# An attention block on one core: GpSimd's memsets of three groups split and placed later, the fourth query block ahead of the next group's keys

## The chip, the core and the metric

The kernel runs on one core of a Trainium2 chip. The metric is the time of one execution on the device, in microseconds. The core has five engines with instruction queues of their own: TensorE (PE, matrix products; its weight loads are listed as PEld), VectorE (DVE), ScalarE (ACT), GpSimd (POOL) and SyncE (SP, which here only issues DMAs). Each engine works through its queue in order; engines wait for each other by semaphores alone.

## What is computed

Multi-head attention with its projections, for 2048 tokens of width 448 and 16 heads of 28 (inputs and output in bf16):

```
qkv = (x @ wqkv).reshape(B, S, 3, H, Dh).transpose(2, 0, 3, 1, 4)
q, k, v = qkv
scores = einsum("bhqd,bhkd->bhqk", q, k) * Dh ** -0.5
p = softmax(scores, axis=-1)
o = einsum("bhqk,bhkd->bhqd", p, v)
return o.transpose(0, 2, 1, 3).reshape(B, S, D) @ wo
```

## The kernel before

**Tiles and windows.** The 16 heads are four groups (g) of four, the queries four blocks (c) of 512. A pair (g, c) is a window w = 4g + c, of which there are 16. A window has 16 rows (128 keys each), a row four score tiles of 128 x 512, one for each head: 1024 tiles in all. Window 0 and window 1 are each cut in two: first four rows of each (tiles 0 to 31), then the other twelve rows of each (to tile 127). Window 2 starts at tile 128, window 3 at 192, and group 1 at 256.

**What becomes of a tile.** PE computes the scores (line 875, `emit_S`). A softmax bound is folded into the product by extra rows of the keys (from NK) and of the queries (from QP), so no maximum is searched. Then there are three ways to the exponential:

- ACT takes two tiles at a time from a PA bank (PSUM has two PA banks) with one instruction, line 1295, into PTA.
- DVE and POOL share a tile from a PD bank (three, and the PO bank at times): DVE makes DU (line 1076) and DV (1079), POOL the product DG (1082), DVE the result PTD (1095). This is `start_tile`; the text calls DG a product.
- POOL makes a tile nearly alone: DVE copies it to SG (1008) and POOL takes six instructions (1015, 1018, 1021, 1023, 1025, 1038). This is `start_g`. Such tiles are taken 10 to 13 rows ahead of the others (`ahead`, LA = 10), and only where their queries and keys are there already.

PE then adds the products with the values into PO (line 1140), where a column of ones in the values (VA) also gives the sum of the exponentials; windows are normalised by way of a small DMA (RRB) and POOL (line 975), and multiplied with `wo`. Values of group g lie in VA[g]: 32 columns a head, of which every eighth is set to 1.0 by a memset of 128 x 256 elements. VA[0]'s memset is on DVE (line 326), those of VA[1] to VA[3] are on POOL (line 459), in one operation `va_ones`.

**The start.** DMAs bring the key weights WK (ACT's queue), x in three blocks XS, the query weights WQ, WV, and the first 512 rows of x transposed (SP's queue). DVE copies WK into a padded form WKP (line 388, `pad_w`), ACT does so for WQ (389). PE transposes XS (424), DVE and ACT bring the transposes to SBUF as XT (435, 437). PE then projects keys (532, `task_K`) and queries (662, `task_Q`) of the first block, ACT and DVE evacuate them (676, 548, 682 to 688), and the first scores and the first exponential follow.

**Who sets the order.** The order of all queues is written out by a planner in the kernel file: a list scheduler that keeps a model time. Operations (`Op`) have an engine, a modelled duration, dependencies, a priority (smaller first) and a condition `elig`, mostly on `pos[0]`, the number of score tiles issued so far. Whatever is ready on a free engine with the smallest priority comes next (`try_static`; for PE `try_pe`). Only the order is taken from it: on the chip an instruction starts when its queue has come to it and its semaphores allow. An operation without dependencies, such as `va_ones`, thus runs as soon as the queue reaches it. `DLAT` and `QLAT` are the modelled times from issue to landing of the key and the query moves (with 0.3 or 0.6 added for the keys), `KSP` the distance in tiles between the projections of the next group's four key blocks, `QPR` what is taken off a query block's priority.

For the first group, key moves are KB<-KB (line 591) and KB<-NK (601); for later groups 613 and 623. A query block w from 2 on is projected into a free bank, evacuated by DVE (672), made absolute (701; for group 0 also scaled, 705), and moved by two DMAs QB<-QB (710) and four QB<-QP (716). The block of w = 3 (the fourth) has priority 168 before the change, and may start at tile 131. The key blocks of group 1 have 56, 92, 128 and 164, and may start at tiles 2, 54, 106 and 158.

Behind `va_ones` stands `halves` (two small memsets, 463 and 464, and two small tensor_scalars, 466), also for POOL, from tile 8 on.

Of the kernel before, what the change touches and what calls it, by code (L numbers as in the profile page):

```python
# [21 lines left out]
RS = 8  # L22
NR = 128 // RS
G = 4
# [29 lines left out]
EVK = 0.66  # L54
RED = 0.59
DISS = 0.6
DLAT = 1.4
QLAT = 2.6
WINDOW = 3.4
BAR = 3600.0  # L60
BAR2 = 1700.0
# [23 lines left out]
def kernel(  # L85
# [7 lines left out]
    nc = tc.nc  # L93
# [21 lines left out]
    NG = 3  # L115
    GMAX = 1
    UK = 30
    KSP = 52
    PGX = 0
    GDEC = 4  # L120
    LA = 10
# [30 lines left out]
    QPR = 100  # L152
# [27 lines left out]
    KP0 = -4395  # L180
    KP1 = -4000
    VE = 16
    UV = 4
    BW = (-1, 2, 0)
    THF = (0, 1, 0, 0)
# [90 lines left out]
    def va_rows(g):  # L276
        return VA[g][:].rearrange("p j h (m e) -> p (j h m) e", e=RS)
# [53 lines left out]
    pos = [0]  # L331
# [7 lines left out]
    def add(op):  # L339
        static[op.eng].append(op)  # L340
        return op

    def bank_task():
        return {"slot": None}

    def acq_d(task, early=False, urgent=1e9):
        def f(t):
            if task["slot"] is not None:
                return True
            free = [s for s in ([o_slot] + d_slots if early or pos[0] >= min(urgent, NT - NTAIL) else [o_slot]) if s.free_at <= t + 1e-9]  # L350
            if not free:
                return False
            s = free[-1]
            s.free_at = 1e18
            task["slot"] = s
            return True
        return f
# [17 lines left out]
    def at(n):  # L375
        return lambda t: pos[0] >= n
# [32 lines left out]
    for b in range(NQC - XBAR):  # L409
        xs_in = add(Op("SP", 0.01, None, prio=-2000 + b, lat=XLAT[b]))  # L410
        for hf in range(2):
# [7 lines left out]
            def tr(b=b, hf=hf, tv=tv, tv2=tv2):  # L419
                for c2 in range(2):  # L420
                    for t in range(TPC):
# [5 lines left out]
                         elig=None if 2 * b + hf < 2 + TE else lambda t: len(k0mm) == 2 * CC and all(o.end is not None for o in k0mm),  # L427
# [15 lines left out]
            else:  # L443
                evo = add(Op(eng, 0.655 if eng == "DVE" else 0.905, ev, deps=[tro], prio=(EVP[b] if b else -5000) + 10 * b + hf,
                             elig=None if b == 0 or eng == 'ACT' or not BW[b] else lambda t, b=b: len(qb0) == HG and qb0[BW[b] - 1].end is not None))
# [8 lines left out]
            nc.sync.dma_start(out=WO[e::RS, :, :],  # L454
                              in_=bass.AP(wo.tensor, wo.offset + e * D, [[(RS - 1) * D, NR], [HG * Dh * D, G], [1, D]]))

    def va_ones():
        for g in range(1, G):
            nc.gpsimd.memset(va_rows(g)[:, :, RS - 1:RS], 1.0)
    add(Op("POOL", 0.9, va_ones, prio=-50, elig=lambda t: pos[0] >= 8))  # L460

    def halves():
        nc.gpsimd.memset(negm[:], 0.0)
# [15 lines left out]
    for g in range(1, G):  # L479
        for (WP, nm, off) in ((WKP, "k", D), (WQP, "q", 0)):  # L480
            def ld(g=g, WP=WP, off=off):
                for cc in range(CC):
# [5 lines left out]
                                      elig=None if first else (lambda t, g=g, nm=nm: pos[0] >= (30 if nm == "q" and g == 1 else (g - 2) * 256 + 120 + 40 * (nm == "q"))), lat=PLT))  # L488
# [29 lines left out]
    def task_K(g, sc):  # L518
# [6 lines left out]
        else:  # L525
            task = bank_task()
            acq = acq_d(task, urgent=(g - 1) * 4 * WT + (sc + 1) * KSP - UK)
            elig = at((g - 1) * 4 * WT + sc * KSP + 2)
            prio = due
# [47 lines left out]
    def task_kmax(g):  # L577
# [7 lines left out]
        if g == 0:  # L585
# [3 lines left out]
            for n, (c0, c1) in enumerate(KCH):  # L589
                for i in range(HG):  # L590
                    o = add(Op("SP", DISS, (lambda i=i, c0=c0, c1=c1: nc.sync.dma_start(
                        out=KB[0][i // 2][HP * SI[i]:HP * (SI[i] + 1), c0 * QW:c1 * QW],
                        in_=KB[1][0][HP * SI[i]:HP * (SI[i] + 1), c0 * QW:c1 * QW])),
                        deps=[k0ev[sc] for sc in range(c0, c1)], prio=-2000 + 20 * n + i, lat=DLAT + 0.3))
                    k0mv.append(o)
# [3 lines left out]
            def rep0(i, c0, c1):  # L599
                st = SI[i] ^ 1  # L600
                nc.sync.dma_start(out=KB[0][i // 2][HP * st:HP * (st + 1), c0 * QW:c1 * QW].rearrange("p (r q) -> p r q", q=P),
                                  in_=NK[0][HP * SI[i]:HP * (SI[i] + 1), None, :].to_broadcast([HP, (c1 - c0) * QW // P, P]))
            for n, (c0, c1) in enumerate(RCH):
                for i in range(HG):
                    o = add(Op("SP", DISS + 0.07, (lambda i=i, c0=c0, c1=c1: rep0(i, c0, c1)), deps=[nk],
                               prio=(-1990 + 20 * n if c0 else -300) + 0.1 * i, lat=DLAT + 0.6, elig=None if c0 else lambda t: pos[0] >= NF * FB * HG + 4))
                    for c in range(c0, c1):
# [4 lines left out]
        for st in (1, 3):  # L612
            o = add(Op("SP", DISS, (lambda st=st: nc.sync.dma_start(
                out=KB[g % 2][1][HP * st:HP * (st + 1), c0 * QW:S], in_=KB[g % 2][0][HP * st:HP * (st + 1), c0 * QW:S])),
                deps=[kev[(g, sc, 0)] for sc in range(c0, NQC)], prio=due + 0.01 * st, lat=DLAT + 0.3))
            deps.append(o)
# [3 lines left out]
        def rep_out(i, c0):  # L620
            st = SI[i] ^ 1
            n = (S - c0 * QW) // P
            nc.sync.dma_start(out=KB[g % 2][i // 2][HP * st:HP * (st + 1), c0 * QW:S].rearrange("p (r q) -> p r q", q=P),
                              in_=NK[g][HP * SI[i]:HP * (SI[i] + 1), None, :].to_broadcast([HP, n, P]))
        nk = add(Op("POOL", 0.25, lambda: nc.gpsimd.tensor_scalar(
            out=NK[g][:], in0=maskm[:, 0:P], scalar1=KMAX[g][:, 0:1], scalar2=0.0, op0=ALU.mult, op1=ALU.add), deps=[m], prio=prio + 0.2, elig=elig))
        for i in (2, 3, 0, 1):
            o = add(Op("SP", DISS + 0.07, (lambda i=i: rep_out(i, c0)), deps=[nk] + ([deps[i]] if i < 2 else []),
                       prio=due + 0.3 + 0.001 * i, lat=DLAT + 0.6))
            for c in range(c0, NQC):  # L630
# [6 lines left out]
    def task_Q(g, c):  # L637
        due = (g * 4 + c) * WT - 24
        n = qabs_n[0] % 2
        qabs_n[0] += 1  # L640
        w = g * 4 + c
        if w == 0:
            task = {"slot": d_slots[1]}
            acq = lambda t: xt_half[1].done(t)
            elig = None
            prio = -4500
        else:
            task = bank_task()
            acq = acq_d(task, urgent=w * WT - UQ)
            elig = at((w - 1) * WT + 3 - (QEA if w > 3 else 0))  # L650
            prio = due - (QPR if w > 3 else 0)
            if w < NF:
                task = {"slot": d_slots[2]}
                acq = lambda t: xt_half[2].done(t)
                elig = None
                prio = Q1P
            elif w == NF:
                acq = acq_d(task, urgent=Q2U)
                elig = at(Q2E)
                prio = 20  # L660
# [12 lines left out]
        if w < NF:  # L673
# [17 lines left out]
            for i in range(HG):  # L691
                o = bound(qb, i, KPART[0], [ab, kmaxop[0][0], e1], pq + (20 if i < 2 else 40) + 0.01 * i)
                if w == 0:
# [5 lines left out]
                    elig=elig if w < NQB else (lambda t: pos[0] >= ((w - NQB + 1) * WT if w - NQB >= NF else NF * FB * HG + (w - NQB + 1) * (WT - FB * HG)))))  # L699
# [9 lines left out]
        for st in (1, 3):  # L709
            mvs[st] = add(Op("SP", DISS, (lambda st=st: nc.sync.dma_start(  # L710
                out=qb[1][HP * st:HP * (st + 1), :], in_=qb[0][HP * st:HP * (st + 1), :])),
                deps=[ev], prio=(Q1M if w < NF else prio - 100) + 0.1 * st, lat=QLAT))
        mine = []
        for i in range(HG):
            st = SI[i]
            o = add(Op("SP", DISS, (lambda i=i, st=st: nc.sync.dma_start(
                out=qb[i // 2][HP * (st ^ 1):HP * ((st ^ 1) + 1), :], in_=QP[n][HP * st:HP * (st + 1), :])),
                deps=[ab] + ([mvs[st ^ 1]] if st in (0, 2) else []), prio=(Q1M + 1 if w < NF else prio - 99) + 0.1 * i, lat=QLAT))
            mine.append(o)
# [3 lines left out]
    def task_V(g, jq):  # L723
        due = g * 4 * WT + jq * TPC * HG - 12 + (FB * HG * (NF - 1) if g == 0 and jq else 0)
        task = bank_task()
        early = False
        elig = at(VE + jq * 5 if g == 0 else (g - 1) * 4 * WT + jq * WT + 4)
        prio = due
        ap = lambda: bank(task)[:]

        def mm(jj):
            for cc in range(CC):
                nc.tensor.matmul(out=ap()[:, jj * GW:(jj + 1) * GW], lhsT=XT[jq][cc // 2][0:CK, cc % 2, jj * P:(jj + 1) * P],  # L733
                                 rhs=WV[:, cc, g * GW:(g + 1) * GW], start=(cc == 0), stop=(cc == CC - 1))
        ops = []
        for jj in range(TPC):
            ops.append(add(Op("PE", 0.27, (lambda jj=jj: mm(jj)), deps=(xt_done[jq] + [wvin]) if jj == 0 else [ops[-1]],
                              prio=prio + 0.001 * jj, kind="W", elig=elig, acq=acq_d(task, early, urgent=due - UV if g == 0 else (g - 1) * 4 * WT + (jq + 1) * WT + 32) if jj == 0 else None,
                              lat=0.0 if jj < TPC - 1 else PLAT)))
# [13 lines left out]
        if g == 0:  # L753
            hot.append((ops[0], due - UV))

# [3 lines left out]
    def open_when(slot, ops):  # L759
# [3 lines left out]
        for o in ops:  # L763
            prev = o.after
            o.after = (lambda t, prev=prev: (prev(t) if prev else None, f(t)))
    task_Q(0, 0)
    open_when(a_slots[0], [xt_half[3]])
    a_slots[1].free_at = 0.0
# [5 lines left out]
    for c in range(1, NQC):  # L774
        task_Q(0, c)
    for g in range(1, G):
        for sc in range(NQC):
            task_K(g, sc)
        task_kmax(g)
        for c in range(NQC):  # L780
            task_Q(g, c)
        for jq in range(NQC):
            task_V(g, jq)
# [556 lines left out]
    while True:  # L1340
        if not times:
            break
        t = heapq.heappop(times)
# [76 lines left out]
    g = G - 1  # L1420
# [43 lines left out]
```

## Time and profile before

| what | value |
|---|---|
| time, median of 3 runs | 414.0 us (413.88 to 415.25) |
| time of the profiled execution | 415.08 us |
| its span in the profile | 413.3 us |
| granted PE clock, mean | 0.989 |
| busy: ACT / DVE / PE / POOL | 395.2 / 382.9 / 360.2 / 340.5 us |
| exponentials on ACT (line 1295) | 422, 1170 ns mean, 16.14 us to 404.54 us |
| products on POOL (line 1082) | 155, 1154 ns mean |
| tiles that POOL makes nearly alone | 26 |

The span is the time that the profile covers. Records of neighbouring instructions of an engine overlap by some hundred ns, so a mean of 1170 ns doesn't mean that one starts each 1170 ns. The page cuts the span in 40 slices of 10.3 us and gives busy tenths. In a windows table each row is a stretch, followed by its length, busy time (and count) of PE, PEld, DVE, ACT, POOL, then the granted PE clock as a share of full speed, the DMA share and GB/s. In the waits, an engine's instruction stands left of the arrow and what it waited for right of it, with the total, the number and the longest. In the timelines and the chain, the first number is the start and the second the duration.

### The profile page before, as it was taken

The page shows a single profiled execution, that of the slowest core. Times are in us where ns is not written, and L with a number is a line of the kernel's source. Part 1 is how long each engine was busy: PE and PEld are TensorE (multiplying, and loading weights), DVE is VectorE, ACT ScalarE, POOL GpSimd, SP SyncE. Part 2 cuts the span into 40 slices and gives each one's busy share as a digit, 9 for nine tenths or more (in the row PEclk, how much of TensorE's full clock was granted, in tenths as well). Part 3 has the DMA queues.
Part 4 walks back from the last instruction along what each step waited for, and adds up shares of the span by engine and source line. Part 5 has one row for each costly group of instructions (what it writes and reads, how often), then busy time and mean ns, then how long its engine had stood idle before and what let it go on. Part 6 is the DMA issues. An engine that isn't in the chain of part 4 may idle for free.

```text
span 413.3 us, 7565 instructions
## 1 busy us (share of the span) xinstructions
PE 360.2 (87%) x2591; PEld 120.9 (29%) x2602; DVE 382.9 (93%) x664; ACT 395.2 (96%) x434; POOL 340.5 (82%) x365
## 2 busy tenths in 40 slices
PE   5999989888898989889898988989798888889995
PEld 2543223222323232232323223232322222222231
DVE  6796899999999999999999999899999999998983
ACT  2799999999999999999999999999999999999993
POOL 6026998879999999899888989978998997989870
PEclk9799999999999999999999999999999999999998
DMA  9233213122101011032101001023100001010112
GB/s 230 22 71 48 55 24 58 22 71 51 52 17 32 21 33 11 15 74 56 48 21 31 3 14 52 12 56 70 34 21 6 26 5 48 2 51 2 51 71 90
DMA packets 36870, 17.30 MB, mean 42 GB/s; under 512 B 29216, under 2 KB 33568, under 8 KB 36832
## 3 DMA queue, kind: packets, MB, share of 16 engines
q1 hardware_dynamic: 36224, 16.61, 17.0%
q8 instruction: 20, 0.33, 0.3%
q10 hardware_dynamic: 608, 0.22, 0.2%
q14 instruction: 18, 0.15, 0.1%
HBM read 6.91 MB, written 2.33 MB: 22 GB/s over the span
## 4 chain that ended last, share of the span: by engine, by line
ACT 36%; DVE 28%; PE 14%; POOL 9%; issue 6%; DMA 4%; SPq 1%; DVEq 0%; POOLq 0%; ACTq 0%
ACT PTA L1295 36%; DVE PTD L1095 7%; DVE DU L1076 7%; DVE DV L1079 7%; PE PA L875 5%; POOL DG L1082 5%; PE PO L1140 3%; DMA RRB<-SCR 2%; POOL GV L1021 1%; DVE SG L1008 1%; PE PD L875 1%; DMA WK<-in_wqkv_dram 1%; POOL OT L975 1%; PE PD L817 1%; DVE QB L672 1%
## 5 line engine op out<-in xcount | busy, mean ns | idle before, releaser
L1295 ACT ACTIVATE PTA<-PA 128x1024 bf16<-128x1024 f32 x422 | 387.7, 1170 | 1.0 <-PE PA L875 0.9
L1082 POOL TENSOR_TENSOR DG<-DV,DU 128x512 f16<-128x512 f16 x155 | 177.0, 1154 | 40.0 <-DVE DV L1079 31.8
L875 PE MATMUL PA<-QB,KB 64*128 64x512 bf16 x843 | 168.9, 380 | 36.4 <-ACT PTA L1295 33.4
L875 PEld LDWEIGHTS <-KB 64*128 64x128 bf16 x1024 | 64.6, 93 | 176.9 <-issue 169.2
L1095 DVE SCALAR_TENSOR_TENSOR PTD<-PD,DG 128x512 uint16<-128x512 f32 x155 | 104.5, 682 | 5.1 <-POOL DG L1082 4.4
L1076 DVE TENSOR_SCALAR DU<-PD 128x512 f16<-128x512 uint16 x155 | 103.0, 681 | 5.0 <-PE PD L875 4.6
L1079 DVE SCALAR_TENSOR_TENSOR DV<-PD,DU 128x512 f16<-128x512 uint16 x155 | 103.7, 682 | 1.0
L1140 PE MATMUL PO<-PTA,VA 128*32 128x512 bf16 x843 | 86.7, 386 | 0.2
L875 PE MATMUL PD<-QB,KB 64*128 64x512 bf16 x181 | 65.9, 377 | 3.0 <-DVE PTD L1095 1.3
L1140 PE MATMUL PO<-PTD,VA 128*32 128x512 bf16 x181 | 52.1, 387 | 0.0
L1140 PEld LDWEIGHTS <-VA 128*32 128x32 bf16 x1024 | 19.7, 94 | 51.5 <-issue 51.1
L1025 POOL TENSOR_TENSOR SG<-SG,GU 128x512 f32<-128x512 f32 x26 | 30.0, 1155 | 2.1 <-DVE QP L701 0.8
L1021 POOL TENSOR_TENSOR GV<-GE,GU 128x512 f16<-128x512 f32 x26 | 30.1, 1157 | 1.5 <-DVE QP L701 0.7
L1023 POOL TENSOR_TENSOR GU<-GV,GU 128x512 f16<-128x512 f16 x26 | 30.0, 1154 | 1.3 <-DVE QP L701 0.4
L1015 POOL TENSOR_SCALAR GU<-SG 128x512 f16<-128x512 uint16 x26 | 16.1, 617 | 7.2 <-DVE SG L1008 3.3
L975 POOL TENSOR_TENSOR OT<-OSB,RRB 128x512 bf16<-128x512 f32 x15 | 19.0, 1269 | 3.1 <-DMA RRB<-SCR 3.1
L1008 DVE COPY SG<-PD 128x512 f32<-128x512 f32 x26 | 17.7, 680 | 3.4 <-PE PD L875 3.4
L662 PE MATMUL PO<-XT,WQP 112*128 112x512 bf16 x56 | 18.1, 385 | 1.0 <-DVE OSB L960 0.6
L733 PEld LDWEIGHTS <-XT 112*128 112x128 bf16 x256 | 13.9, 98 | 13.1 <-issue 12.8
L1018 POOL TENSOR_SCALAR GE<-SG 128x512 f32<-128x512 uint16 x26 | 16.1, 618 | 2.1
L1038 POOL TENSOR_SCALAR PTD<-SG 128x512 uint16<-128x512 f32 x26 | 16.1, 619 | 1.5 <-PE PD L875 0.6
L733 PE MATMUL PO<-WV,XT 112*128 112x112 bf16 x192 | 15.5, 214 | 0.9 <-DVE QB L672 0.5
(108 smaller groups left out, 206.6 us busy)
## 6 DMA issues: line engine op xcount, KB each, us to landing
RRB<-SCR SPq DMA_DIRECT2D x15, 256.0 KB, 3.3
QB<-QP SPq DMA_DIRECT2D x56, 32.0 KB, 1.8
KB<-NK SPq DMA_DIRECT2D x12, 128.0 KB, 2.7
XS<-in_x_dram SPq DMA_DIRECT2D x3, 448.0 KB, 4.7
QB<-QB SPq DMA_DIRECT2D x28, 32.0 KB, 1.8
out_dram<-XS SPq DMA_DIRECT2D x2, 448.0 KB, 2.9
KB<-KB SPq DMA_DIRECT2D x6, 128.0 KB, 2.3
RRB<-RR SPq DMA_DIRECT2D x2, 256.0 KB, 3.4
```

The lines of the kernel that those rows point to most:

```text
L733: nc.tensor.matmul(out=ap()[:, jj * GW:(jj + 1) * GW], lhsT=XT[jq][cc // 2][0:CK, cc % 2, jj * P:(jj + 1) * P], rhs=WV[:, cc, g * GW:(g + ...
L875: nc.tensor.matmul(out=ap, lhsT=KB[g % 2][i // 2][a:a + 64, j * P:(j + 1) * P], rhs=QB[w % NQB][i // 2][a:a + 64, :], start=True, stop=Tru ...
L975: o5 = add(Op("POOL", 1.22, lambda: nc.gpsimd.tensor_tensor(out=OT[g][c][:], in0=OSB[b][:], in1=RRB[b][:], op=ALU.mult), deps=o4, prio=-10 ...
L1021: g3 = add(Op("POOL", PTT, lambda: nc.gpsimd.tensor_tensor(out=GV[:], in0=GE[:], in1=GU[:], op=ALU.mult), deps=[g2], prio=prio + 2, kind=" ...
L1023: g4 = add(Op("POOL", PTT, lambda: nc.gpsimd.tensor_tensor(out=GU[:], in0=GV[:], in1=GU[:], op=ALU.mult), deps=[g3], prio=prio + 3, kind=" ...
L1025: g5 = add(Op("POOL", PST, lambda: nc.gpsimd.tensor_tensor(out=X[:], in0=X[:], in1=GU[:], op=ALU.add), deps=[g4], prio=prio + 4, kind="g", ...
L1076: p1 = add(Op("DVE", P1, lambda: nc.vector.tensor_scalar(out=DU[b][:], in0=lo, scalar1=SIG / 65536, scalar2=SIG * (SS - 0.5), op0=ALU.mult ...
L1079: p2 = add(Op("DVE", P1, lambda: nc.vector.scalar_tensor_tensor(out=DV[b][:], in0=lo, scalar=65536 * (SS - 0.5 + CE / C3), in1=DU[b][:], o ...
L1082: gq = add(Op("POOL", PTT, lambda: nc.gpsimd.tensor_tensor(out=DG[b][:], in0=DV[b][:], in1=DU[b][:], op=ALU.mult), deps=[p2], prio=n, kind ...
L1095: f = add(Op("DVE", P1, lambda: nc.vector.scalar_tensor_tensor(out=PTD[st["s"].idx][:].bitcast(U16), in0=PX[slot.idx][:], scalar=EBITS + C ...
L1140: nc.tensor.matmul(out=PO[HP * st:HP * (st + 1), :], lhsT=VA[g][:, j, st, :], rhs=r["p"][i][1](), start=first, stop=last, tile_position=(0 ...
L1295: nc.scalar.activation(out=PTA[pslot.idx][:, 0:len(ns) * QW], in_=PA[s.idx][:, 0:len(ns) * QW], func=ACT.Exp, bias=ACT_BIAS, scale=ACT_SCALE)
```

## The change

Three things are edited. The memsets of VA[1], VA[2] and VA[3] become three operations, each with a modelled duration of 1.17 instead of 0.9 for all, which may start when 24, 48 and 72 score tiles are issued instead of 8. The query block w = 3 gets 100 taken off its priority, as later ones had already (68 instead of 168). And three constants of the planner are new: DLAT 2.1 instead of 1.4, QLAT 2.0 instead of 2.6, KSP 60 instead of 52, so that the key blocks of group 1 may start at tiles 2, 62, 122 and 182.

```diff
-DLAT = 1.4
-QLAT = 2.6
+DLAT = 2.1
+QLAT = 2.0
...
-    KSP = 52
+    KSP = 60
...
+    VON = 24
...
-    def va_ones():
-        for g in range(1, G):
-            nc.gpsimd.memset(va_rows(g)[:, :, RS - 1:RS], 1.0)
-    add(Op("POOL", 0.9, va_ones, prio=-50, elig=lambda t: pos[0] >= 8))
+    for g in range(1, G):
+        add(Op("POOL", 1.17, lambda g=g: nc.gpsimd.memset(va_rows(g)[:, :, RS - 1:RS], 1.0), prio=-50 + g, elig=lambda t, g=g: pos[0] >= VON * g))
...
-            prio = due - (QPR if w > 3 else 0)
+            prio = due - (QPR if w > 2 else 0)
```

## The prediction

> **What bounds the kernel now.** I read the page first, for the engine that has no slack.
>
> ```profile
> PE 360.2 (87%) x2591; PEld 120.9 (29%) x2602; DVE 382.9 (93%) x664; ACT 395.2 (96%) x434; POOL 340.5 (82%) x365
> ...
> ACT  2799999999999999999999999999999999999993
> POOL 6026998879999999899888989978998997989870
> PEclk9799999999999999999999999999999999999998
> ```
>
> ScalarE (ACT) is full from the third slice to the last but one. The waits of ACT, longest first, show where its idle time is:
>
> ```profile
> ACT QB L676 <- PE PD L662: 6.3, 1, 6.3
> ...
> ACT PTA L1295 <- PE PA L875: 0.9, 2, 0.5
> ```
>
> Once the exponentials (L1295) run, they wait for 0.9 us in all. They begin at 16.14 and end at 404.54, 422 of them, so one each 0.920 us. The span is therefore: start (16.1) + exponentials (388.4) + tail (8.8). A change pays only if it moves the first exponential, the number of exponentials, or the tail. So I looked at the start next, in the chain of waits in order of time:
>
> ```profile
> 0.74 4.31 DMA WK<-in_wqkv_dram
> 5.04 0.21 issue
> 5.25 0.38 DVE WKP L388
> 5.63 2.73 issue
> 8.37 0.68 DVE XT L435
> 9.05 0.04 issue
> 9.09 1.01 PE PD L532 x2
> ```
>
> The padded key weights arrive, VectorE (DVE) copies them, and then 2.73 us pass with no named wait before the next copy. The timelines of DVE and of GpSimd (POOL) for 4.6 to 9 us (start, duration, instruction) say what went on:
>
> ```profile
> 5.25 3.19 DVE L388 COPY WKP<-WK 112x448 bf16<-112x448 bf16 x1 [0.77 <-DMA WK<-in_wqkv_dram]
> ```
>
> ```profile
> 4.64 3.51 POOL L459 MEMSET VA<- 128x256 bf16 x3
> 7.73 0.47 POOL L463 MEMSET negm<- 128x64 bf16 x1
> 8.02 0.30 POOL L464 MEMSET FW<- 128x128 bf16 x1
> 8.29 0.37 POOL L466 TENSOR_SCALAR negm<-maskm 128x16 bf16<-128x16 bf16 x2
> ```
>
> L388 copies SBUF to SBUF and takes 3.19 us. ACT does the same shape (L389) in 0.56, and L684 on DVE, a 128x512 copy with POOL idle, takes 0.29. It ends at 8.44, 0.29 us after the third memset of VA (8.15). So the three memsets, which nobody needs yet, hold up the first link of the start. There is a second price: TensorE (PE) has nothing from 5.93 to 9.09, and the windows table shows its granted clock fall.
>
> ```profile
> 8.00:8.50 0.50, 0.00 (x0) 0.00 (x1) 0.50 (x2) 0.00 (x0) 0.50 (x5) 0.94 1.17 224
> 8.50:9.00 0.50, 0.00 (x0) 0.10 (x1) 0.50 (x2) 0.00 (x0) 0.16 (x1) 0.50 2.24 194
> ...
> 15.00:15.50 0.50, 0.50 (x10) 0.50 (x9) 0.47 (x2) 0.50 (x1) 0.00 (x0) 0.74 0.00 0
> ```
>
> The clock (third number from the end) is half from about 8.44 to 15.26 (0.94 and 0.74 as shares of their half microseconds). The whole preparation of the first scores runs in that stretch.
>
> **The change, part by part.**
>
> *Memsets.* By the rule in the code, the first of the three is placed once 24 score tiles are issued. Before the first PD score matmul (25.80) PE has issued 22; the next pair passes 24, 2 us before the first product (28.20). So I read VON = 24 as: memset 1 still stands ahead of the first product in POOL's queue, memsets 2 and 3 behind some. Nothing in front of memset 1 waits for data, so it runs early, but now after the four small instructions (L463, L464, L466 twice). These take 0.93 us from the start of the first to the end of the last (7.73 to 8.66), so from 4.64 to at latest 5.57. In the old run the copy got through among just these four (it ended at 8.44, they at 8.66). I take it that it does so again, ahead of memset 1: end 5.57 + 0.29 = 5.86, 2.58 us earlier.
>
> Then, link by link. The XT copy starts at 5.79, the first projection matmul at 6.5 instead of 9.09. PE's gap is then 5.93 to 6.5, and I take the clock to stay full. The eight projection matmuls took 9.09 to 12.66 (0.43 each and a gap); at full clock two matmuls of L532 at 19.05 start 0.21 apart, so they end at about 6.5 + 8 x 0.21 = 8.2, with 0.2 for the second XT copy 8.4: 4.3 earlier. The 32 transposes behind them in PE's queue took 3.09 (12.66 to 15.75); at the rate of the last eight (0.53) 2.12, so they end at 10.5. Their data is there: the last XS load lands 6.5 us after its issue at about 2.2, at 8.7. On ACT the way from QB (12.70) to the end of the second KB (15.64) is 2.94 us of its own work: 8.44 + 2.94 = 11.4. DVE's bounds come out 2.0 us behind QB's start (14.67), now 10.4. First scores at 10.6, first exponential at the latest of these, 11.4 instead of 16.14: 4.7 less. Behind it everything shifts alike, if the loads are there: WV landed at 9.9 and the DMA share is 0 from 13.5 on, while the last key projection would run at 16 instead of 20.8. I keep 4.6. Bounds of this part: 0, if the stall was not the memsets' doing, and 5.0, if the copy passes all four small ones. If the cover of the later steps is gone, late next are ACT's own four instructions ahead of the first exponential, which no earlier copy shortens.
>
> The Trainium skill ("SBUF — State Buffer", section Who interferes with whom) says that such a copy and a GpSimd instruction exclude each other, and that the one that begins first keeps the port pair for the whole instruction. The trace agrees on the exclusion, but the old copy also lost at two borders between memsets (5.9 and 7.0), so the rule alone doesn't say who wins the border at 5.3 to 5.6.
>
> *The memsets behind products.* Two land at tiles 48 and 72, so around 34 and 43 us at 0.379 us a tile (388.4 / 1024). There POOL is full: 40 to 50 us shows 9.35 of 10. They take 1.14 us from start to start, at most 1.56 each: 2.3 to 3.1 us of POOL. A tile made by POOL alone costs it 5.3 us (0.62 + 0.62 + 1.16 + 1.15 + 1.16 + 0.62) and saves ACT 0.46 (half of 0.920), so 2.3 us is 0.44 tile, +0.20 us, at most +0.27. Queued behind each memset is a product DG, its DVE step, and a PD bank for PE; ACT stands one PA bank away from that, so a delay of 1.2 us there need not reach it.
>
> *Fourth query block first.* Its projection runs at 76.27, its six DMAs (two of QB<-QB, four of QB<-QP, 0.55 each on SP) at 80.8 to 86.35. The windows table:
>
> ```profile
> 75.00:80.00 5.00, 3.90 (x20) 1.04 (x16) 5.00 (x10) 5.00 (x6) 5.00 (x5) 1.00 0.24 24
> 80.00:85.00 5.00, 4.17 (x30) 1.53 (x29) 5.00 (x11) 5.00 (x7) 2.14 (x3) 1.00 0.17 37
> 85.00:90.00 5.00, 4.13 (x37) 1.46 (x37) 4.31 (x9) 5.00 (x7) 3.63 (x4) 1.00 0.42 118
> ```
>
> POOL (fifth pair) idles 2.86 + 1.37 = 4.2 us there: it starts no tile of its own 10 rows ahead, because those rows need the fourth block. Moved ahead of the keys, block and tile come earlier; SP's queue is empty from 66.1 to 76.25, so the DMAs pass nothing. Worth at most 4.2 / 5.3 = 0.8 tile, -0.37 us; at worst the keys behind it come 3 us later (they land at 96.8, their window begins at tile 256, 113 us), 0. I take -0.2, which cancels the memsets.
>
> *DLAT, QLAT, KSP.* They change no instruction, only the order: key moves are now counted 0.7 us slower (2.4 and 2.7 against 2.3 and 2.7 to landing), query moves 0.6 faster (2.0 against 1.8), keys wait 8 to 24 tiles more. The trace can't price a new order. Bounds by the count of exponentials: four more or fewer of 422, +-3.7 us. I take 0, since the old order already leaves ACT only 0.9 us idle.
>
> **Sum.** The profiled execution took 415.08 us, 1.78 of it outside its span, and is 1.1 over the median of 414.0. 415.08 - 4.6 + 0.2 - 0.2 = 410.5; from the median it is 409.4, if the 1.1 isn't in the start. I forecast 410.0, between the two.
>
> **Rivals.**
> 1. *The copy waits for memset 1.* If this one wins the border, it holds DVE from about 5.3 to 6.5 (1.25, the first one's row), the copy ends at 6.8 and PE starts at 7.45. Speaks for it: two borders lost before. PE is then busy for 1.9 of the 3.4 us to 8.44; if the clock falls all the same, 4.6 matmuls are through, the rest and the first transposes run at half: Q ends at 9.9 instead of 12.66, 2.75 gained, 412.3 by the profiled execution, 411.3 by the median. The skill ("TensorE: Matmul & The Clock Gate", What's actually happening) throttles after an idle window; PE is not idle in this one, and by that it keeps full speed, Q ends at 9.2, 3.5 gained, 410.5 to 411.6. The old stretch 5.03 to 8.44 had 0.9 us of work and fell all the same, so the rule is loose here.
> 2. *It doesn't do what it says.* The stall wasn't the memsets', or the small four alone keep it up: 414.0, within 0.3%. For: the record of L326 on DVE (5.36 to 5.63) lies inside that of L388, so the records are not clean. Against: L684 at 0.29, and the end beside the memset's.
> 3. *Slower, by the new order.* Counted 0.7 us slower, the first keys (KB<-KB issued at 22.87, scores of tile 32 at about 30) make the planner see PD tiles later, where DVE already idles 3.4 us at 37 to 40, and the two memsets push products there. Each PD tile lost is +0.46 us on ACT. Decides from ten lost (4.6) on; at thirteen it is 415.4. Against: 181 such tiles over 390 us, one in 2.2 us, so thirteen is 28 us without any.
> 4. *More than forecast*: start gain whole and three exponentials fewer: 407.3.
>
> **Chances.** Forecast 0.46, rival 1 0.25, rival 2 0.12, rival 3 0.11, rival 4 0.06. A measurement of this kernel tells about 0.3% (1.24 us) from no change. Faster by more: forecast, rival 4 and most of rival 1, 0.75; within: rival 2 and the rest of rival 1, 0.14; slower: 0.11. The likeliest case alone is 409.0 to 411.2. For 8 in 10, with the order's +3.7 on the forecast or on rival 1: 408.4 to 414.0.
>
> **What would show it.** L388 at 0.3 to 0.6 us (forecast) or 1.5 (rival 1); first L532 matmul at 6.5 or 7.4; granted clock 1.00 through 8.4 to 15; first L1295 at 11.4 or 13.4; one VA memset before 8 us on POOL; fourth QB evacuation near 67 to 72 and POOL busier at 80 to 90; exponentials 418 to 426. I am wrong if L388 still takes 3 us, if the first exponential moves and the number of L1295 rises by five or more, or if ACT gets idle time behind 18 us.

## The result and the profile after

The changed kernel takes 410.57 us (median of 4 runs, 410.27 to 411.56) against 414.03 us before; the ratio is 0.9914, with a 95% interval of 0.9889 to 0.9939, so 0.6 to 1.1% faster. The forecast was 410.0, its likeliest case 409.0 to 411.2. Two more measurements of the same kernel (below) gave 0.9902 and 0.9910. The profiled execution took 410.69 us, 4.4 less than that of before. One execution of e10 (419.28 us, at a mean clock of 0.754) and one of e12 (419.53 us, at 0.975) ran in a slower state and are left out below.

Line numbers up to 182 are the same in both kernels, those from 183 to 456 one higher, most later ones one lower (the exponentials are L1294 now). First the page of the changed kernel:

```profile
PE 358.8 (88%) x2595; PEld 120.7 (30%) x2606; DVE 380.7 (93%) x664; ACT 395.5 (97%) x434; POOL 341.0 (83%) x365
...
ACT  4999999999999999999999999999999999999994
POOL 5049998899898999989899998979979989989950
PEclk9999999999999999999999999999999999999999
```

ACT does the same work as before (395.5 against 395.2 us), in a span of 408.5 instead of 413.3. The gain stands in the first two slices (2 and 7 before, 4 and 9 now), and the clock no longer has a slice under 9. Its waits:

```profile
ACT QB L675 <- PE PD L661: 1.7, 1, 1.7
...
ACT PTA L1294 <- PE PA L874: 0.4, 2, 0.2
```

The wait for the first query block fell from 6.3 to 1.7 us. The timelines of DVE and POOL for the same stretch show why (start, duration, instruction):

```profile
5.25 0.48 DVE L389 COPY WKP<-WK 112x448 bf16<-112x448 bf16 x1 [0.77 <-DMA WK<-in_wqkv_dram]
5.84 0.69 DVE L436 COPY XT<-PD 112x1024 bf16<-112x1024 bf16 x1
```

```profile
4.64 0.16 POOL L462 MEMSET negm<- 128x64 bf16 x1
4.72 0.22 POOL L463 MEMSET FW<- 128x128 bf16 x1
4.90 0.88 POOL L465 TENSOR_SCALAR negm<-maskm 128x16 bf16<-128x16 bf16 x2
5.64 1.29 POOL L459 MEMSET VA<- 128x256 bf16 x1
```

The copy takes 0.48 us instead of 3.19. It came among the two small tensor_scalars, which now have 0.88 us together instead of 0.37, and ahead of the one memset of VA that still runs early (its record begins 0.09 us before the copy's ends; records overlap that much). The copy's record starts at 5.25 in both kernels, released by the arrival of WK, so what held it before was no semaphore: that engines wait for each other by semaphores alone, as the description of the core has it, leaves this kind of waiting out. The chain in order of time goes from matmul to matmul now, with no "issue" piece of 2.73 us in it:

```profile
1.26 3.57 PE PA L404 x8
4.83 1.40 PE PD L425 x12
6.23 0.43 PE PA L425 x4
6.66 0.54 PE PD L531 x2
7.20 0.22 PE PD L661
7.41 0.43 PE PD L531 x2
7.84 0.66 PE PD L661 x3
8.53 0.70 ACT QB L675
```

And the windows table has a full clock where it was half (third number from the end):

```profile
8.00:8.50 0.50, 0.50 (x6) 0.30 (x4) 0.50 (x1) 0.00 (x0) 0.00 (x0) 1.00 1.54 216
8.50:9.00 0.50, 0.50 (x12) 0.50 (x11) 0.39 (x3) 0.47 (x1) 0.00 (x0) 1.00 3.20 196
...
15.00:15.50 0.50, 0.50 (x4) 0.11 (x2) 0.47 (x2) 0.50 (x2) 0.00 (x0) 1.00 0.00 0
```

The whole account in one table, from the exponentials' line and the timelines of ACT:

| kernel, profiled execution | copy | first exponential | exponentials | last one ends | us each | tail | span |
|---|---|---|---|---|---|---|---|
| before | 3.19 | 16.14 | 422 | 404.54 | 0.920 | 8.8 | 413.3 |
| changed | 0.48 | 11.35 | 422 | 400.45 | 0.922 | 8.1 | 408.5 |

The start gives 4.8 us, the middle takes back 0.7 (389.1 against 388.4), the tail gives 0.7.

### The profile page after: what moved, and what is told of

Its sections match the earlier page's. It is cut to its first block, busy times and chain, and to the rows that moved or that the text cites. A ratio compares the mean times of both kernels' runs of the same rounds, so it can differ in the third digit from the quotient of the medians.

```text
span 408.5 us, 7585 instructions
## 1 busy us (share of the span) xinstructions
PE 358.8 (88%) x2595; PEld 120.7 (30%) x2606; DVE 380.7 (93%) x664; ACT 395.5 (97%) x434; POOL 341.0 (83%) x365
## 4 chain that ended last, share of the span: by engine, by line
ACT 43%; DVE 34%; PE 10%; issue 6%; POOL 4%; DMA 1%; DVEq 0%; SPq 0%; POOLq 0%; ACTq 0%
ACT PTA L1294 43%; DVE DU L1075 8%; DVE DV L1078 8%; DVE PTD L1094 8%; PE PA L874 3%; PE PO L1139 3%; POOL DG L1081 2%; DVE KB L566 1%; DVE SG L1007 1%; PE PD L874 1%; DVE KPART L570 1%; DVE VA L748 1%; DMA RRB<-SCR 1%; PE PA L404 1%; DVE DRC L968 1%
## 5 line engine op out<-in xcount | busy, mean ns | idle before, releaser
L1294 ACT ACTIVATE PTA<-PA 128x1024 bf16<-128x1024 f32 x422 | 388.0, 1175 | 0.9 <-PE PA L874 0.4
L1139 PE MATMUL PO<-PTA,VA 128*32 128x512 bf16 x843 | 85.5, 386 | 0.7 <-DVE QB L671 0.4
L1139 PE MATMUL PO<-PTD,VA 128*32 128x512 bf16 x181 | 55.6, 386 | 0.3
L1139 PEld LDWEIGHTS <-VA 128*32 128x32 bf16 x1024 | 19.9, 94 | 50.0 <-issue 48.7
L1014 POOL TENSOR_SCALAR GU<-SG 128x512 f16<-128x512 uint16 x26 | 16.1, 617 | 5.5 <-DVE SG L1007 3.1
L1017 POOL TENSOR_SCALAR GE<-SG 128x512 f32<-128x512 uint16 x26 | 16.1, 618 | 2.9 <-DVE QP L700 1.0
L1037 POOL TENSOR_SCALAR PTD<-SG 128x512 uint16<-128x512 f32 x26 | 16.1, 619 | 1.9 <-DVE KPART L570 0.5
L531 PE MATMUL PO<-XT,WKP 112*128 112x512 bf16 x48 | 15.5, 385 | 0.4 <-DVE OSB L959 0.4
```

The lines of the kernel that those rows point to most:

```text
L1139: nc.tensor.matmul(out=PO[HP * st:HP * (st + 1), :], lhsT=VA[g][:, j, st, :], rhs=r["p"][i][1](), start=first, stop=last, tile_position=(0 ...
L1294: nc.scalar.activation(out=PTA[pslot.idx][:, 0:len(ns) * QW], in_=PA[s.idx][:, 0:len(ns) * QW], func=ACT.Exp, bias=ACT_BIAS, scale=ACT_SCALE)
```

## The experiments

The theory: all of the gain is the start, and it comes because nothing long runs on GpSimd when the key weights arrive; the new latencies, KSP and the fourth block bring nothing. The rivals: the new order has a part in it; or the copy waits for any memset in the queue. The number of exponentials of a kernel can be counted in the order that its planner writes out, before it runs. e1 to e8 ran on one chip, e9 to e12 on another, each beside the kernel before, which then measured 414.88 (e1 to e4), 414.16 (e5 to e8) and 414.22 us (e9 to e12).

### The two halves of the change: e1 and e2

e1 is the kernel before with the memset edit alone:

```diff
+    VON = 24
...
-    def va_ones():
...
-    add(Op("POOL", 0.9, va_ones, prio=-50, elig=lambda t: pos[0] >= 8))
+    for g in range(1, G):
+        add(Op("POOL", 1.17, lambda g=g: nc.gpsimd.memset(va_rows(g)[:, :, RS - 1:RS], 1.0), prio=-50 + g, elig=lambda t, g=g: pos[0] >= VON * g))
```

> The kernel before with the memset edit alone (three operations, at tiles 24, 48 and 72); DLAT, QLAT, KSP and the fourth query block as before. It has 421 exponentials on ACT, one fewer than before. Theory (the whole gain is the start, freed by the memsets): VectorE's copy of WK at 0.4 to 0.6 us, first exponential near 11.4, time as that of the changed kernel, 410.6, or 0.9 less for the exponential fewer: 409.6 to 410.6. Rival (the new order carries a good part): 412 or more, though the start moves.

Measured: 408.75 us, ratio 0.9854 (0.9835 to 0.9873), below what was expected. Copy 0.48 us, first exponential at 11.2, last end 398.94, tail 7.9. The memset edit alone brings more than the whole change.

e2 is the changed kernel with the old single operation `va_ones` back in it, so the other half.

> The changed kernel with the old single memset operation, so that only DLAT, QLAT, KSP and the fourth query block are changed. It has 423 exponentials, one more than before. Theory: the copy of WK still takes 3.2 us, the first exponential starts at 15 to 16.2, and the time is that of before, 414.0, or 0.9 more: 414.0 to 415.0. Rival (the order carries part): 413 or less.

Measured: 415.87 us, ratio 1.0031 (1.0018 to 1.0043). Copy 3.16 us, first exponential at 15.9, 423 of them. That is above the expected range. The other half by itself costs 1.0 us, and one exponential is 0.92. So the rival that the new order brings part of the gain falls; but the theory's "bring nothing" falls too, since the order is a cost.

### What the copy waits for: e3 and e6

e3 is the kernel before with one number changed, so that the four small instructions stand ahead of the three memsets, all of them still ahead of the first product:

```diff
-    add(Op("POOL", 0.8, halves, prio=-49, elig=lambda t: pos[0] >= 8))
+    add(Op("POOL", 0.8, halves, prio=-51, elig=lambda t: pos[0] >= 8))
```

> The kernel before with one number changed: the operation with the four small GpSimd instructions stands ahead of the three memsets, which stay together, all ahead of the first product. 422 exponentials in an unchanged order. Theory (what counts is what GpSimd runs when the weights arrive at 5.25; the copy passes the small ones and gets in ahead of the first memset): copy 0.5 us, first exponential 11.4, 410.5. Rival (the copy waits as long as memsets follow one upon the other): copy 3 us, first exponential near 16, 414.0. Between them, if it loses to the first memset only: copy 1.5 us, 411.5 to 412.5.

Measured: 411.17 us, ratio 0.9937 (0.9904 to 0.9970), but the twelve runs fall in two groups: seven of 409.99 to 411.19 and five of 414.72 to 416.06. The profiled execution is one of the first group. Its timelines, DVE and POOL:

```profile
5.26 0.49 DVE L388 COPY WKP<-WK 112x448 bf16<-112x448 bf16 x1 [0.77 <-DMA WK<-in_wqkv_dram]
```

```profile
4.66 0.16 POOL L463 MEMSET negm<- 128x64 bf16 x1
4.74 0.22 POOL L464 MEMSET FW<- 128x128 bf16 x1
4.92 0.95 POOL L466 TENSOR_SCALAR negm<-maskm 128x16 bf16<-128x16 bf16 x2
5.82 3.52 POOL L459 MEMSET VA<- 128x256 bf16 x3
```

The same three memsets, run early and back to back, cost nothing here: the copy was through before the first of them. So it isn't the number of memsets early on that counts, nor that they stand ahead of the products, but what POOL runs when the copy becomes ready at about 5.3 us. That the five late runs are those in which the copy came second is inferred from their times (near those of before), not seen in a trace.

e6 turns it round: VA[1] and VA[2] ahead of the small four, VA[3] at tile 72, otherwise the changed kernel.

```diff
-... prio=-50 + g, elig=lambda t, g=g: pos[0] >= VON * g))
+... prio=-60 + g, elig=lambda t, g=g: pos[0] >= (8 if g <= 2 else VON * g)))
```

> The changed kernel with the memsets of VA[1] and VA[2] in front of the four small instructions, VA[3] at tile 72 as changed. 423 exponentials, one more. Theory (the copy waits until the second memset is through): copy of WK ends near 7.3 (2.0 us), first projection near 7.9. If TensorE's clock falls all the same, as in the kernel before: first exponential near 13.9, time 413.5 to 414.3. If it stays full, since TensorE then works again before the stretch is over: first exponential near 12.8, time 412.5 to 413.2. Rival (any of the memsets held it, two as much as three): copy 3 us, 415.

Measured: 413.78 us, ratio 0.9983 (0.9967 to 0.9999). The copy takes 2.06 us and ends at 7.33: two memsets, then the copy, as expected; three took 3.19, none ahead 0.48. The first exponential stands at 14.3. The windows of this kernel:

```profile
7.50:8.00 0.50, 0.02 (x1) 0.02 (x1) 0.50 (x2) 0.00 (x0) 0.05 (x1) 0.79 1.08 266
8.00:8.50 0.50, 0.50 (x2) 0.22 (x2) 0.26 (x1) 0.00 (x0) 0.00 (x0) 0.50 3.36 194
...
11.00:11.50 0.50, 0.50 (x6) 0.35 (x5) 0.32 (x2) 0.02 (x1) 0.00 (x0) 0.79 1.18 229
```

The clock falls at 7.79 (0.79 as a share of half a microsecond) and is back at 11.21. In the profile of before it fell at 8.44, so the moment isn't the same in each execution (the last section shows what it follows). Here PE began again at 7.98, too late for this one. The runs spread from 412.19 to 414.60. A half clock of 3.4 us leaves a mean of 0.996 (this profile's); two of the twelve runs, 412.19 and 412.45, have 0.998 and 1.000, so in these the clock can't have fallen for that long. Both branches of the expectation seem to occur.

### The clock by itself: e4

The kernel before, with 12 matmuls of zeros into a PA bank not yet in use behind the first block's transposes; the memsets stay as they were.

```diff
+            if b == 0 and hf == 1:
+                tro0 = tro
...
+    def fill():
+        for n in range(12):
+            warm(n)
+    add(Op("PE", 0.01, fill, deps=[tro0], prio=-4998, kind="T"))
```

> The kernel before with 12 matmuls of zeros (into a PA bank that nothing uses yet) behind the first block's transposes, so that TensorE is busy while VectorE's copy is held up; the memsets stay as before. Theory (the start lost 2.6 us to the copy and about 2.1 to the half clock behind it): copy still 3.2 us, granted clock full from 8.4 to 15, first projection at 9.1, first exponential near 14.0, time 1 to 2 us under before: 412 to 413. Rival (the clock costs nothing, since ACT and VectorE set the pace): first exponential 16, 414.0.

Measured: 412.87 us, ratio 0.9955 (0.9938 to 0.9973); 2.0 us less than before. Timelines of DVE and of PE, and a row of the windows table:

```profile
5.26 3.23 DVE L388 COPY WKP<-WK 112x448 bf16<-112x448 bf16 x1 [0.77 <-DMA WK<-in_wqkv_dram]
```

```profile
5.63 2.75 PE L403 MATMUL PA<-zrow,zeros 128*128 128x512 bf16 x12
```

```profile
8.50:9.00 0.50, 0.00 (x0) 0.10 (x1) 0.50 (x1) 0.00 (x0) 0.21 (x2) 1.00 3.88 183
```

The copy is held up just as before, and the clock stays full. The first exponential starts at 13.9 (14.0 expected). The 4.8 us of the start are thus 2.3 us of clock (16.14 to 13.88) and 2.5 us of the copy (13.88 to 11.35). Executions of the kernel before say the same without an edit: two of the 57 beside e1 to e12 have a mean clock of 0.999, so no half clock of 3.4 us, and they take 412.25 and 412.36 us, some 2 us less than its medians.

### The changed kernel against its parts: e5, e9, e10, e12

e5 and e10 are the changed kernel again; e9 is the memset edit alone again, beside e10; e12 is the kernel before with the fourth block's priority alone (the edit of `QPR`).

> The changed kernel as it is, beside the next three, to compare it with the memset edit alone (408.75) by way of the kernel before. 422 exponentials. Theory: time 410.3 to 410.8; and, since its first memset of VA stands right behind the four small instructions, an execution in which the copy of WK loses that one border shows 1 to 1.5 us more (one of four has shown 411.6). Rival (the difference of 1.8 us to the memset edit alone comes from the runs, not from the kernels): 409.5 or less.

> The memset edit alone again, now on the same chip as the changed kernel (next). 421 exponentials against 422. Theory (the two differ by one exponential and little else): 0.7 to 1.5 us less than the changed kernel. Rival (equal, the earlier difference came from the runs): within 0.4 us.

> The changed kernel, beside the memset edit alone. Theory: 0.7 to 1.5 us above it; 409.9 to 410.7. Rival: within 0.4 us of it.

> The kernel before with the fourth query block's priority alone changed. 423 exponentials. Theory of the prediction (GpSimd gets its idle time near 80 to 90 back, worth 0.2 us): 414 or a little less, GpSimd busier at 80 to 90. Rival (the time goes by the number of exponentials, whatever GpSimd's idle time there): 0.9 above the kernel before, 414.8 to 415.6.

Measured: e5 409.99 us, ratio 0.9902 (0.9886 to 0.9919), runs of 409.66 to 410.30. That lies between the theory's range and the rival's. None of the five is longer by 1 us, so a lost border was not caught; the run of 411.56 us among the first four left no trace. e9 408.64 us, ratio 0.9874 (0.9855 to 0.9892); e10 410.22 us (five runs), ratio 0.9910 (0.9890 to 0.9929). Beside each other on one chip the memset edit alone is thus 1.6 us faster than the whole change. One exponential would account for 0.9 of it, the tail (7.9 against 8.1 in e5) for 0.2; what the rest is stays open. e5's profile (span 407.6, against 406.8 of e9) shows only 0.8 in all, but the spans of e10's five runs go from 407.4 to 408.9, those of e9 from 406.8 to 407.2, and none of those five was profiled.

e12: 415.02 us (eleven runs, of 413.29 to 418.45), ratio 1.0027 (1.0004 to 1.0049), 423 exponentials. The rival's range holds, though the loss is barely clear of the noise; the gain of 0.2 us that the prediction gave the block doesn't show. The fourth block isn't even earlier. Its evacuation in the DVE timelines of before, of e12, and of e1, in which its priority is the old one:

```profile
78.53 0.74 DVE L672 TENSOR_SCALAR QB<-PO,offscol 128x512 bf16<-128x512 f32 x1
```

```profile
77.77 0.74 DVE L672 TENSOR_SCALAR QB<-PO,offscol 128x512 bf16<-128x512 f32 x1
```

```profile
65.92 0.74 DVE L671 TENSOR_SCALAR QB<-PO,offscol 128x512 bf16<-128x512 f32 x1
```

Counted from the first exponential (16.1, 15.5, 11.2) these are 62.4, 62.3 and 54.7 us. The priority alone moves nothing; the new place of the memsets moved the block by 7.7 us, without its priority being touched. In the changed kernel it is at 66.06, 54.7 behind the first exponential, the same place.

### All three behind products: e7, e8, e11

e7 is the changed kernel with VON = 40; e8 the kernel before with the memset edit at VON = 40 and KSP = 60; e11 the kernel before with the memset edit at tiles 32, 48 and 72. In all three no memset of VA runs before the first product, so the border at 5.3 us is gone.

> The changed kernel with VON 40 instead of 24, so that all three memsets of VA stand behind the first two products. 421 exponentials, one fewer. Theory: copy of WK 0.4 to 0.5 us in every execution, first exponential 11.2 to 11.4, time 0.9 less than the changed kernel, 409.4 to 409.9, and no executions 1 us longer. Rival (the memset behind products delays a product and ACT): ACT waits for scores for more than 1 us, 411 or more.

> The kernel before with the memset edit at VON 40 and KSP 60; DLAT, QLAT and the fourth query block as before. 421 exponentials; all three memsets behind the first two products. Theory (start as in the changed kernel, 421 exponentials, and the old latencies leave the end as it was): 408.6 to 409.5, below both kernels. Rival (the new latencies and the fourth block help by themselves): 410 or more.

> The kernel before with the memset edit alone, its three operations at tiles 32, 48 and 72, so that all stand behind the first product. 420 exponentials. Theory (first exponential 11.2, 0.92 us an exponential, a tail of 8): 0.9 less than the memset edit alone, 407.5 to 408.2, if ACT's waits for PE stay under 0.7 us. Rival (as in the two kernels with all three behind the first two products, the new order puts a wait of 1.9 us on ACT near 68 us): 409.5 to 410.1.

Measured: e7 411.19 us, ratio 0.9934 (0.9917 to 0.9950); e8 411.02, 0.9930 (0.9914 to 0.9946); e11 410.57, 0.9919 (0.9902 to 0.9937). All have the early start (first exponential at 11.2, copy 0.47 to 0.48) and fewer exponentials (421, 421, 420), and all are slower than e1: each of the three theories forecast too little, by 1.3 us or more. The waits of ACT, e7 and then e11:

```profile
ACT PTA L1294 <- PE PO L1139: 1.9, 1, 1.9
```

```profile
ACT PTA L1294 <- PE PO L1139: 1.2, 1, 1.2
ACT PTA L1294 <- PE PA L874: 1.0, 1, 1.0
```

ACT waits once for 1.9 us (near 68 us) in e7, and 2.2 us in two (at 85.6 and 88.7) in e11; e8 has the same wait as e7. In both, PE's queue holds a long run of products with the values (L1139) in PO and no scores for ACT. In e7 that run waits for DVE to evacuate a query block from PO (timeline of PE, e7):

```profile
69.20 0.38 PE L1139 MATMUL PO<-PTA,VA 128*32 128x512 bf16 x1 [0.67 <-DVE QB L671]
```

In e11 the fourth block is evacuated only at 81.35, 70 us behind the first exponential, and window 3 needs it from tile 192 on (11.2 + 192 x 0.379 = 84); the waits of ACT come right then. That the late block is their cause is argued from these times, not tested. The rivals' numbers for e7 (411 or more) and e8 (410 or more) came out, but by another path than they named: ACT has no wait over 0.3 us near the memsets at 26, 45 and 59 us, and in e8 neither the latencies nor the block were changed. e11 came out above its rival's range too.

## Why the prediction was right, and where it wasn't

**What bounds the kernel.** Start, exponentials and tail: held. A change of order shows in the number of exponentials, 0.92 us each (e2, e12: one more, 1.0 and 0.8 us), or as idle time of ACT (e7, e11).

**The copy and the memsets.** Held in cause and size: no stall where nothing long stands ahead (0.48, against an end forecast at 5.86 it ended at 5.73), first projection 6.59 (6.5 forecast), first exponential 11.35 (11.4), one memset of VA early, two among the products at 31.3 and 42.1 (34 and 43 in the prediction, which counted them from the old start). The last link held as well: ACT's own way from QB at 8.53 to the first exponential took 2.82 us (2.94). The times of e3 suggest that the border of rival 1 is a real one, lost by the copy in 5 of 12 runs; in the changed kernel, where one memset stands behind it, no trace shows a loss.

**The clock.** Held: 2.3 us in e4 against the 2.1 that the sum leaves beside the copy's 2.58. It took the clock for full from the start, though; in the changed kernel's profile it was half until 6.66 (last section), so the transposes ended at 6.66 instead of 5.93. By luck this cost little: the second XT copy started at 6.70 instead of 6.47 (e1), and the first exponential came 0.15 us later than in e1. In e6 PE had worked until 5.6, so for 1.2 of the 3.4 us before the fall at 7.79, and the clock fell all the same; it then stayed half for 3.4 us. The Trainium skill's rule ("TensorE: Matmul & The Clock Gate", What's actually happening) of an idle window that throttles is too narrow here.

**From the profiled execution to the median.** The forecast split the difference of 1.1 us, 410.5 or 409.4. The 57 runs of before beside e1 to e12 suggest what it was: on the whole, the lower their mean clock, the longer they take. Those at 0.988 average 415.5 us, at 0.992 414.5, at 0.996 414.1, at 0.999 412.3. The profiled execution (0.989, with 6.8 us of half clock) is one of the slower. So part of the 1.1 was probably in the start, and the median gained 3.5 rather than 4.8. This is inferred from means, which also count a fall behind the last matmul (at 411.21 in the profile of before). 410.5 was the better end.

**The memsets among products, +0.2; the fourth block, -0.2; the order, 0.** In sum right, term by term not. The fourth block's priority moved nothing alone (e12), and the POOL time that was to come back at 80 to 90 us did come back, but from the memset edit, and another idle stretch appears at 65 to 75. The windows tables of before and of the changed kernel (the other rows of before stand in the prediction):

```profile
65.00:70.00 5.00, 4.47 (x43) 1.48 (x41) 5.00 (x9) 5.00 (x6) 3.90 (x5) 1.00 0.37 64
70.00:75.00 5.00, 5.00 (x51) 1.51 (x44) 4.54 (x9) 5.00 (x7) 4.92 (x6) 1.00 0.01 3
```

```profile
65.00:70.00 5.00, 4.73 (x40) 1.41 (x39) 4.96 (x10) 5.00 (x6) 3.08 (x4) 1.00 0.08 20
70.00:75.00 5.00, 4.57 (x46) 1.64 (x45) 4.96 (x9) 5.00 (x7) 3.88 (x5) 1.00 0.25 38
75.00:80.00 5.00, 4.27 (x25) 1.56 (x25) 4.97 (x10) 5.00 (x6) 4.68 (x6) 1.00 0.12 14
80.00:85.00 5.00, 4.05 (x30) 1.23 (x29) 4.93 (x10) 5.00 (x7) 4.71 (x5) 1.00 0.24 70
85.00:90.00 5.00, 5.00 (x50) 1.57 (x50) 4.96 (x10) 5.00 (x6) 4.88 (x6) 1.00 0.12 31
```

POOL's idle time at 80 to 90 us fell from 4.2 to 0.4 us, that at 65 to 80 rose from 1.2 to 3.4, so 1.6 us of the 3.8 are kept. The longest pause, of 1.9 us, sits where the fourth block now is evacuated (66.06, then its two small DVE steps at 67.32 and 68.12; POOL starts again at 68.55, behind the second): part of the idle time moved with the block.

And the order was not worth 0: the latencies, KSP and the priority cost 1.0 us alone (e2) and 1.6 beside the memset edit (e9 against e10). The bounds of four exponentials either way were too wide in number (420 to 423 in all kernels) and left out the form that cost more, a wait of ACT of 1.9 to 2.2 us. That the forecast came so near is thus in part luck: the memset edit alone brought 5.6 to 6.1 us (e9, e1), over 1 us more than the 4.4 that the sum gives it, and the rest of the change took about as much back.

**A version better than both.** The memset edit alone, with the planner's constants as they were: 408.75 and 408.64 us, 0.9854 (0.9835 to 0.9873) and 0.9874 (0.9855 to 0.9892) of before.

## What to carry to other kernels

An instruction that nobody waits for can still stand in the way: look at what a neighbour engine runs at the moment when the first link of the start becomes ready, and read a plain copy that takes many times its usual length as a copy that is held up. A stall ahead of matmuls is paid twice if the clock falls in it (here 2.5 us of stall and 2.3 of half clock); a filler on the idle engine (e4) prices the second payment separately. Where a written-out order is changed together with a fix, measure the fix alone: here the rest of the change gave back 1.6 us of 5.6.

## What was not expected of the hardware

The copy on DVE that became ready while POOL ran memsets back to back didn't get in between two of them: 2.06 us with two ahead, 3.19 with three, 0.48 with none; among the small instructions of about 0.2 us it got in. The Trainium skill ("SBUF — State Buffer", Who interferes with whom) speaks of one instruction that keeps the port pair; in this case a whole row of them kept the copy out.

The granted clock of the windows table reads 1.00 from the first microsecond on, yet the first matmuls L404 start 0.43 us apart, twice the 0.21 of full clock. The clock records in the traces begin only later, at 5.02 us in the profile of before and at 6.66 in that of the changed kernel, and the transposes show that PE ran at half until then: in before they start about 0.11 us apart up to 5.04 and half as far apart from there on, in the changed kernel all 16 start about 0.11 apart (PE timelines, before and then changed):

```profile
4.68 1.02 PE L424 MATMUL PD<-ident,XS 128*112 128x128 bf16 x12
```

```profile
4.71 1.53 PE L425 MATMUL PD<-ident,XS 128*112 128x128 bf16 x12
```

So the column says nothing ahead of its first record; the spacing of the matmuls does. And the fall follows the rise: in each of the four profiles in which the clock falls during the start, it falls 3.4 us after the first record (before 5.02 and 8.44, e2 4.41 and 7.82, e6 4.38 and 7.79, e12 5.72 and 9.14). The rise itself wanders between executions of one kernel, though the first matmul starts near 1.26 in all: 6.66 and 4.90 in two of the changed kernel (the second is e5's), 6.18 and 4.66 in two with the memset edit alone (e1, e9). That would let a kernel such as e6 lose the clock in one execution and keep it in another; no pair of traces of one kernel shows both.
